# Loading batch 1 ahead of w_in, bringing the first keys as bf16, and cutting the first scores by 384 columns, in a fused attention and feed-forward kernel on one Trainium2 core

## The chip, the cores and the metric

The kernel runs on one core of one Trainium2 chip. The metric is the device time of one execution in microseconds (us), and lower is better. Every execution is listed as undisturbed ("fast"). Kernels are compared only within the same rounds.

A core has five engines with their own instruction streams: TensorE (PE in the profile) for matmuls, ScalarE (ACT) for exponentials, VectorE (DVE), GpSimd (POOL), and SyncE (SP), which only issues transfers. Each engine runs its own stream in program order. Transfers run on 16 DMA engines. A transfer issued by GpSimd can change the type on the way (f32 to bf16), and this queue is called the "cast queue" below.

## The reference, cut to what matters

```python
# q [8,16,384,64], k and v [8,4,384,64], w_in [1024,2048], w_out [2048,1024], all float32
k, v = repeat(k, 4, axis=1), repeat(v, 4, axis=1)   # 16 query heads share 4 key heads
attn = softmax(q @ k.T / 8) @ v                     # per batch and head
x = attn.transpose(0, 2, 1, 3).reshape(3072, 1024)
h = maximum(x @ w_in, 0)
out = (h * h) @ w_out                               # float32 [3072,1024]
```

## The kernel before

One program does attention and feed-forward for 8 batches. The attention of a batch has 4 key groups of 3 key blocks each, 12 units of 128 keys by 4 heads. It first needs k and q transposed ("turned"): kT and qT have the head dimension on the partitions. For batches 0 and 1 the turns run on TensorE against an identity matrix, with a copy by VectorE behind each. From batch 2 on they are transposing transfers. Scores go to PSUM, ScalarE makes exponentials of them, and the product with v ("v product") follows on TensorE. The result is turned once more and goes through w_in ("up" matmuls) and w_out ("down" matmuls).

The program isn't written in its final order. A recorder keeps a model clock for each engine and each queue. At every step the main loop picks the next piece of TensorE work by the model's time at which it would be ready, and among ready pieces by priority. The order of the matmuls is therefore fixed when the program is built. On the chip TensorE then executes that order.

```python
# Recorder.add: what the model believes of a transfer and of an instruction
if dma is not None:
    self.clock[eng] = start + issue
    q = eng
    begin = max(self.ring.get(q, 0.0), start + issue + 0.8)   # queue is serial
    self.ring[q] = begin + cost
    end = begin + cost + 1.2
else:
    self.clock[eng] = start + cost
    end = start + cost + (0.2 if eng == "tensor" else 0.07)
```

The first loads, in the order of the queues:

```python
keys("sync", 0, 1)                       # key group 0 of batch 0 as f32
# ScalarE's queue: q heads 0-3 as f32 (one transfer), then key groups 1-3 as f32
keys("scalar", 1, HKV)
# cast queue (GpSimd), f32 to bf16:
load_q(0, 4, 8)
...                                      # identity matrix
load_v(0)
load_q(0, 8, 12)
load_q(0, 12, 16)
for g in range(1, HKV):
    dup_k(0, "gpsimd", g, g + 1)         # each key block twice side by side, k_dup
aug_v(0, "gpsimd")
for i in range(3):
    load_w_in(i)                         # 1 MB of f32 each, 512 KB as bf16
load_k(1)
load_q(1, 0, 8)
load_q(1, 8, 16)
load_v(1)
for i in range(3, 8):
    load_w_in(i)
dup_k(1, "gpsimd")
aug_v(1, "gpsimd")
```

The scores of batch 0 go in 18 small bursts through two pairs of PSUM banks (1024 columns each, as 2x512 or 2x2x256), each with one exponential of 128x1024. Later batches use bursts with exponentials of 128x3072.

```python
for u in range(NU):
    smalls.append([(u, 0)])
    if u % 2 == 1:
        smalls.append([(u - 1, 512), (u, 512)])
...
# main loop: candidates (model time when ready, priority, what); the lowest priority that is ready wins
if turn_q:
    b, g, w = turn_q[0]
    ...
    cand.append((max(R.when(reads=src), open_bank(spare)), 1, "turn"))
...  # v products 2, turns of the output 3, scores of b0 priority 0, of others 4, up and down 5
ready = [x for x in cand if x[0] <= now + 0.05]
what = min(ready, key=lambda x: x[1]) if ready else min(cand)
```

The softmax here doesn't subtract the row's maximum and nothing guards it: scores larger than these inputs give would overflow.

Of the kernel before, what the change touches and what calls it, by code (L numbers as in the profile page):

```python
# [8 lines left out]
class Recorder:  # L9
# [35 lines left out]
    def add(self, eng, fn, reads=(), writes=(), dma=None, cost=0.1, issue=0.1, rate=None):  # L45
        i = len(self.ops)
# [19 lines left out]
        if dma is not None:  # L66
            self.clock[eng] = start + issue
            q = eng
            begin = max(self.ring.get(q, 0.0), start + issue + 0.8)
            self.ring[q] = begin + cost  # L70
            end = begin + cost + 1.2
        else:
            self.clock[eng] = start + cost
            end = start + cost + (0.2 if eng == "tensor" else 0.07)
# [59 lines left out]
def bass_gqa_attention__then__ffn_squared_relu_kernel(  # L134
# [33 lines left out]
    k_f32 = sb("k_f32", [128, NU, D], f32)  # L168
# [31 lines left out]
    def load_k(b, after=()):  # L200
        st = b % NST
        R.add("gpsimd", lambda g: g.dma_start(  # L202
            k_st[st].ap().rearrange("p (g j) d -> p g (j d)", g=HKV),
            k[b].rearrange("g (p j) d -> p g (j d)", j=NJ)),
            reads=after, writes=[("k_st", st)], dma=f"k{st}", cost=1.3, issue=0.8)

    def first_loads():

        def keys(eng, g0, g1):
            R.add(eng, lambda e: e.dma_start(  # L210
                k_f32[:, g0 * NJ:g1 * NJ, :].rearrange("p (g j) d -> p g (j d)", j=NJ),
                k[0, g0:g1].rearrange("g (p j) d -> p g (j d)", j=NJ)),
                writes=[("k_f32", g) for g in range(g0, g1)], dma=f"kf{g0}", cost=0.4 * (g1 - g0), issue=0.4)

        keys("sync", 0, 1)
        R.add("scalar", lambda e: e.dma_start(
            q_f32[:, :, :], q[0, 0:4].rearrange("h (p j) d -> p h (j d)", j=NJ)),
            writes=["q_f32"], dma="qf", cost=1.3, issue=0.4)
        keys("scalar", 1, HKV)
# [8 lines left out]
    def load_q(b, h0, h1):  # L228
# [4 lines left out]
            writes=[("q_st", st, h // 4, x) for h in range(h0, h1, 4) for x in range(2)], dma=f"q{st}_{h0}",  # L233
# [19 lines left out]
    def dup_k(b, eng, g0=0, g1=HKV):  # L253
        n = (g1 - g0) * NJ
        src = (k_st[b % NST] if b else k_f32)[:, g0 * NJ:g1 * NJ, :].unsqueeze(2).to_broadcast([128, n, 2, D])
        dst = k_dup[b % 2][:, g0 * NJ:g1 * NJ, :, :]
        R.add(eng, lambda e: e.tensor_copy(dst, src), reads=[("k_st", b % NST)] if b else [("k_f32", g) for g in range(g0, g1)],  # L257
# [7 lines left out]
    def turn_k_dma(b):  # L265
# [3 lines left out]
            writes=[("kT", b % 2, g) for g in range(HKV)], dma="turn_k", cost=2.0)  # L269

    def turn_q_dma(b, half):
# [4 lines left out]
            writes=[("qT", b % 2, 2 * half + i, x) for i in range(2) for x in range(2)], dma=f"turn_q{half}", cost=2.5)  # L276
# [16 lines left out]
    def turn_q_pe(b, g, banks, t0=0, t1=6):  # L293
# [3 lines left out]
        parts = [h for h in range(2) if t0 < (4, 6)[h] and t1 > (0, 4)[h]]  # L297

        def tr(pe):
            for t in range(t0, t1):  # L300
# [8 lines left out]
              reads=[("bank", i)], writes=[("qT", b % 2, g, h) for h in parts], cost=0.07 + 0.068 * (t1 - t0))  # L309


    def score_reads(b, u, parts=(0, 1)):
        g = u // NJ
        return [("kT", b % 2, g)] + [("qT", b % 2, g, h) for h in parts]
# [5 lines left out]
    def burst_small(b, pieces, base):  # L320

        wide = 512 // len(pieces)

        def sc(pe):
            for n, (u, c0) in enumerate(pieces):
                for x in range(2):
                    m = pe.matmul(ps[:, base + x, n * wide:(n + 1) * wide],  # L327
                                  kT[b % 2][64 * x:64 * x + 64, u, :], q_cols(b, u // NJ, x, c0, c0 + wide))
            return m

        keys = [("bank", base), ("bank", base + 1)]
        R.add("tensor", sc, reads=[r for u, c0 in pieces for r in score_reads(b, u, (c0 // 512,))], writes=keys,
              cost=0.22 + 0.19)
        n, c0 = (b * NU + pieces[0][0]) % NEX, pieces[0][1]
        src = ps[:, base:base + 2, :].rearrange("p x (k c) -> p x k c", k=len(pieces))
# [370 lines left out]
```

## Time and profile before

| | before |
|---|---|
| median of the first 3 executions | 432.33 us |
| span of the profiled execution | 430.6 us |
| TensorE busy | 421.8 us (98%) |
| first exponential starts, last of the 18 ends | 6.94, 24.43 us |
| first exponential of batch 1 (128x3072) starts | 33.31 us |

The summary page of the kernel before (first line and engine busy times; the last is each engine's busy time, its share and its instructions) says that TensorE is nearly always busy:

```profile
span 430.6 us, 7790 instructions
...
PE 421.8 (98%) x3428; PEld 231.6 (54%) x3454; DVE 158.9 (37%) x335; ACT 194.0 (45%) x190; POOL 55.6 (13%) x68
```

So only the start can give something. The windows table of the kernel before gives, for each stretch, its length and the busy time of each engine with the count of instructions; then the clock that TensorE was granted as the records have it, the DMA share and the GB/s:

```profile
5.00:10.00 5.00, 4.53 (x34) 2.56 (x34) 2.27 (x7) 3.02 (x4) 3.63 (x7) 1.00 1.22 145
10.00:15.00 5.00, 3.65 (x49) 1.84 (x48) 1.86 (x5) 4.56 (x6) 5.00 (x7) 1.00 1.09 139
15.00:20.00 5.00, 4.77 (x80) 2.90 (x76) 3.47 (x11) 5.00 (x7) 4.25 (x5) 1.00 1.47 197
20.00:25.00 5.00, 4.70 (x75) 2.75 (x74) 2.04 (x7) 4.43 (x5) 1.47 (x1) 1.00 1.60 191
25.00:30.00 5.00, 4.50 (x73) 3.54 (x69) 3.99 (x13) 0.98 (x2) 2.61 (x4) 1.00 1.48 198
```

ScalarE's timeline of the kernel before (start, length, engine, line, operation, tiles, count, idle time before with what ended it) shows the 18 exponentials almost gapless:

```profile
6.94 3.08 ACT L337 ACTIVATE expT<-ps 128x1024 bf16<-128x1024 f32 x3 [1.85 <-PE ps L327]
10.33 14.10 ACT L337 ACTIVATE expT<-ps 128x1024 bf16<-128x1024 f32 x15 [0.30 <-PE ps L327]
```

And TensorE's timeline of the kernel before shows what it does between the bursts, and when batch 1 is turned (first and last of four pairs of turns shown; L426 is an up matmul, L285 a turn of k, L301 one of q):

```profile
19.65 0.49 PE L426 MATMUL ps<-xT,w_in_sb 128*128 128x384 bf16 x2
...
20.39 0.50 PE L426 MATMUL ps<-xT,w_in_sb 128*128 128x384 bf16 x2
...
21.15 0.82 PE L426 MATMUL ps<-xT,w_in_sb 128*128 128x384 bf16 x4
...
28.38 0.33 PE L285 MATMUL ps<-ident,k_dup 128*128 128x128 bf16 x3
28.54 0.50 PE L301 MATMUL ps<-ident,q_st 128*128 128x128 bf16 x6
...
29.88 0.33 PE L285 MATMUL ps<-ident,k_dup 128*128 128x128 bf16 x3
30.06 0.51 PE L301 MATMUL ps<-ident,q_st 128*128 128x128 bf16 x6
```

Eight up matmuls (1.3 us at 0.1625 us each) already sit in the gaps at 19.6 to 21.9 us. Batch 1 is turned after the last exponential, from 28.4 to 30.6 us.

### The profile page before, as it was taken

What the parts mean: (1) busy time and instruction counts of PE and PEld (TensorE: products, weight loads), DVE (VectorE), ACT (ScalarE), POOL (GpSimd) and SP (SyncE); (2) the same over time, 40 slices, a digit from 0 to 9 for tenths busy, and PEclk for the clock granted to TensorE, in tenths of its full rate; (3) what the DMA queues carried; (4) which work ended last, traced back from release to release, by engine and by line L of the source; (5) the groups of instructions that cost most, each with busy time, mean ns of one, the idle gap of its engine ahead of it and who ended that gap; (6) DMA issues with size and microseconds to landing.
All of it is one profiled execution on the core that took longest, in us unless ns stands there. A gap on an engine that the chain in (4) does not pass through costs nothing.

```text
span 430.6 us, 7790 instructions
## 1 busy us (share of the span) xinstructions
PE 421.8 (98%) x3428; PEld 231.6 (54%) x3454; DVE 158.9 (37%) x335; ACT 194.0 (45%) x190; POOL 55.6 (13%) x68
## 2 busy tenths in 40 slices
PE   8899999999999999999999999999999999999997
PEld 4465555465454655546555455645564455446544
DVE  3474422254233543225433243533342144224412
ACT  4937750557545576455773549540241034003300
POOL 7752002404040031004000000000000000000000
DMA  8999999999596189299553230042101100110012
GB/s 147 182 195 202 190 198 215 200 191 138 105 175 156 37 137 131 85 144 166 60 103 94 70 85 0 2 106 69 49 2 49 73 26 1 50 73 26 1 63 85
DMA packets 95331, 43.90 MB, mean 102 GB/s; under 512 B 75712, under 2 KB 89280, under 8 KB 95296
## 3 DMA queue, kind: packets, MB, share of 16 engines
q0 software_dynamic: 36544, 17.44, 32.3%
q1 hardware_dynamic: 57824, 25.27, 26.4%
q10 hardware_dynamic: 928, 0.69, 0.5%
q8 instruction: 27, 0.44, 0.4%
q14 instruction: 8, 0.07, 0.1%
HBM read 35.65 MB, written 12.58 MB: 112 GB/s over the span
## 4 chain that ended last, share of the span: by engine, by line
PE 92%; ACT 3%; DMA 2%; DVE 1%; SPq 1%; issue 1%
PE ps L426 39%; PE ps L471 37%; PE ps L347 7%; PE ps L372 7%; ACT expT L337 3%; DMA qT<-q_st 1%; DMA q_f<-in_q_dram 1%; PE ps L301 1%; SPq L266 1%; DVE o_sb L387 1%; PE ps L327 0%; PE ps L285 0%; DVE qT L308 0%; DVE y_sb L480 0%; DVE rinv L381 0%
## 5 line engine op out<-in xcount | busy, mean ns | idle before, releaser
L426 PE MATMUL ps<-xT,w_in_sb 128*128 128x384 bf16 x1024 | 174.5, 326 | 0.0
L471 PE MATMUL ps<-w_out_sb,h2T 128*128 128x512 bf16 (+2 forms) x758 | 167.7, 375 | 1.7 <-issue 0.5
L357 ACT ACTIVATE expT<-ps 128x3072 bf16<-128x3072 f32 x42 | 114.5, 2725 | 70.9 <-PE ps L347 70.0
L426 PEld LDWEIGHTS ps<-xT,w_in_sb 128*128 128x128 bf16 x1024 | 97.0, 98 | 69.3 <-issue 6.2
L436 ACT ACTIVATE h2T<-hr 128x384 bf16<-128x384 f32 x128 | 64.4, 520 | 138.0 <-DVE hr L434 137.8
L471 PEld LDWEIGHTS ps<-w_out_sb,h2T 128*128 128x128 bf16 x784 | 73.6, 98 | 87.9 <-issue 6.0
L434 DVE TENSOR_SCALAR hr<-ps 128x384 f32<-128x384 f32 x128 | 71.2, 557 | 103.9 <-PE ps L426 103.9
L480 DVE COPY y_sb<-ps 128x512 f32<-128x512 f32 (+2 forms) x49 | 33.3, 681 | 130.7 <-PE ps L471 130.7
L372 PEld LDWEIGHTS ps<-v_aug,expT 128*128 128x128 bf16 x1152 | 39.8, 97 | 6.7 <-issue 0.7
L372 PE MATMUL ps<-v_aug,expT 128*128 128x65 bf16 x1152 | 41.4, 193 | 0.3 <-ACT expT L337 0.3
L387 DVE TENSOR_TENSOR o_sb<-ps,rinv 128x384 bf16<-128x384 f32 x64 | 35.6, 557 | 2.4 <-DVE rinv L381 0.2
L347 PE MATMUL ps<-qT,kT 64*128 64x512 bf16 (+1 forms) x336 | 34.6, 325 | 0.5 <-DMA qT<-q_st 0.5
L347 PEld LDWEIGHTS ps<-qT,kT 64*128 64x128 bf16 x336 | 13.0, 94 | 21.2 <-DVE o_sb L387 4.9
L381 DVE RECIPROCAL rinv<-ps 128x6 f32<-128x6 f32 x64 | 12.1, 190 | 25.5 <-PE ps L372 25.5
L337 ACT ACTIVATE expT<-ps 128x1024 bf16<-128x1024 f32 x18 | 16.9, 1070 | 2.4 <-PE ps L327 2.2
L262 POOL COPY v_aug<-v_st 128x768 bf16<-128x768 bf16 x8 | 6.6, 830 | 83.7 <-PE ps L372 67.8
L230 POOL DMA_DIRECT2D q_st<-in_q_dram x17 | 15.0, 896 | 0.9 <-POOLq L691 0.8
L257 POOL COPY k_dup<-k_st 128x1536 bf16<-128x1536 bf16 x7 | 10.3, 1469 | 37.1 <-DMA k_st<-in_k_dram 37.1
L202 POOL DMA_DIRECT2D k_st<-in_k_dram x7 | 5.3, 757 | 39.9 <-DMA qT<-q_st 39.9
L327 PE MATMUL ps<-qT,kT 64*128 64x512 bf16 (+1 forms) x48 | 7.5, 360 | 1.8 <-ACT expT L337 1.3
L240 POOL DMA_DIRECT2D w_in_sb<-in_moe_w_in_dram x8 | 7.1, 935 | 0.0
L223 POOL DMA_DIRECT2D v_st<-in_v_dram x8 | 6.3, 788 | 0.1
(26 smaller groups left out, 42.8 us busy)
## 6 DMA issues: line engine op xcount, KB each, us to landing
out_dram<-y_sb SPq DMA_DIRECT2D x47, 256.0 KB, 2.0
q_st<-in_q_dram POOLq DMA_DIRECT2D x14, 384.0 KB, 8.9
w_in_sb<-in_moe_w_in_dram POOLq DMA_DIRECT2D x8, 512.0 KB, 16.1
w_out_sb<-in_moe_w_out_dram POOLq DMA_DIRECT2D x4, 1024.0 KB, 26.4
v_st<-in_v_dram POOLq DMA_DIRECT2D x8, 192.0 KB, 9.8
k_st<-in_k_dram POOLq DMA_DIRECT2D x7, 192.0 KB, 3.9
q_st<-in_q_dram POOLq DMA_DIRECT2D x3, 192.0 KB, 5.7
xT<-o_sb SPq DMA_TRANSPOSE x28, 2.8
```

What stands on the lines that cost most here:

```text
L230: R.add("gpsimd", lambda g: g.dma_start(q_st[st][:, h0:h1, :], q[b, h0:h1].rearrange("h (p j) d -> p h (j d)", j=NJ)), writes=[("q_st", st ...
L337: R.add("scalar", lambda e: e.activation(dst, src, AF.Exp, scale=0.125), reads=keys, writes=[("expT", (n + m) % NEX, c0 // 512) for m in r ...
L347: m = pe.matmul(flat[:, k0 * HC + c0:k0 * HC + c1], kT[b % 2][64 * x:64 * x + 64, u + k0, :], q_cols(b, (u + k0) // NJ, x, c0, c1))
L357: R.add("scalar", lambda e: e.activation(dst, src, AF.Exp, scale=0.125), reads=keys, writes=[("expT", (n + m) % NEX, h) for m in range(2) ...
L372: m = pe.matmul(po[:, f - 6 * s2, 0:D + 1], w, v_aug[b % 2][:, g * NJ + j, 0:D + 1], start=(j == 0), stop=(j == NJ - 1))
L381: R.add("vector", lambda e: e.reciprocal(rinv[r].ap().unsqueeze(2), po[:, :, D:D + 1]), reads=[("bank", i)], writes=[("rinv", r)], cost=0.13)
L387: R.add("vector", lambda e: e.tensor_tensor(dst, srcv, rbv, ALU.mult), reads=[("bank", i), ("rinv", r)], writes=[("o_sb", o, s2)], cost=0.48)
L426: m = pe.matmul(bank(i)[:, 0:S], w_in_sb[:, kc, c * 128:(c + 1) * 128], xT[b % NXT][:, kc, :], start=(kc == 0), stop=(kc == NKC - 1))
L434: R.add("vector", lambda e: e.tensor_scalar_max(hr[r][:, :], bank(i)[:, 0:S], 0.0), reads=[("bank", i)], writes=[("hr", r)], cost=0.48)
L436: R.add("scalar", lambda e: e.activation(h2T[b % 2][:, c, :], hr[r][:, :], AF.Square), reads=[("hr", r)], writes=[("h2T", b % 2, c)], cost ...
L471: m = pe.matmul(bank(i)[:, 0:n], h2T[b % 2][:, c, i3 * 128:(i3 + 1) * 128], w_out_sb[:, c, c0:c1], start=(c == 0), stop=(c == NFC - 1))
L480: R.add("vector", lambda e: e.tensor_copy(ysl, bank(i)[:, 0:n]), reads=[("bank", i)], writes=[("y", yb)], cost=0.08 + n / 960)
```

## The change

The intent: (1) load k and q of batch 1 ahead of most of w_in, and turn them in the gaps of batch 0; (2) let key groups 1 to 3 of batch 0 come as bf16 through the cast queue, first in that queue, instead of as f32 through ScalarE's queue; (3) load and cast q group 0 by pairs of heads; (4) cut the first and last scores by 384 columns, so that dependencies are finer (16 bursts of 768 and 6 of 1024 in place of 18 of 1024); (5) tell the model that transposing transfers are slow while the cast queue is busy.

```diff
 # Recorder.add
             begin = max(self.ring.get(q, 0.0), start + issue + 0.8)
+            if shared and self.ring.get("gpsimd", 0.0) > begin:
+                self.ring["gpsimd"] += cost
+                cost = shared
             self.ring[q] = begin + cost
-            end = begin + cost + 1.2
+            end = begin + cost + (1.5 if begin > 30 else 1.2)
 # turn_k_dma, turn_q_dma, turn_o_dma
-dma="turn_k", cost=2.0)
+dma="turn_k", cost=1.4, shared=8.0)
 ...
 # first loads
-        R.add("scalar", lambda e: e.dma_start(q_f32[:, :, :], q[0, 0:4]...
-        keys("scalar", 1, HKV)
+        for n in range(2):
+            R.add("scalar", lambda e, n=n: e.dma_start(q_f32[:, 2 * n:2 * n + 2, :], q[0, 2 * n:2 * n + 2]...
 ...
     first_loads()
+    load_k(0)                       # key groups 1-3 of b0, bf16, first in the cast queue
     load_q(0, 4, 8)
     ...
     load_q(0, 12, 16)
-    for g in range(1, HKV):
-        dup_k(0, "gpsimd", g, g + 1)
+    dup_k(0, "gpsimd", 2, 3)
+    load_k(1)
+    dup_k(0, "gpsimd", 3, 4)
+    load_q(1, 0, 8)
     aug_v(0, "gpsimd")
-    for i in range(3):
+    load_q(1, 8, 16)
+    for i in range(2):
         load_w_in(i)
-    load_k(1)
-    load_q(1, 0, 8)
-    load_q(1, 8, 16)
     load_v(1)
-    for i in range(3, 8):
+    for i in range(2, 4):
         load_w_in(i)
     dup_k(1, "gpsimd")
+    for i in range(4, 8):
+        load_w_in(i)
     aug_v(1, "gpsimd")
 ...
     dup_k(0, "vector", 0, 1)
     # casts of q heads 0-1 and 2-3, now both by VectorE
+    dup_k(0, "vector", 1, 2)        # key group 1, ahead of every later VectorE copy
 ...
 # bursts
-        smalls.append([(u, 0)])
-        if u % 2 == 1:
-            smalls.append([(u - 1, 512), (u, 512)])
+        if NJ < u < NU - NJ - 1:
+            ... as before (wide)
+        elif u in (NJ, NU - NJ - 1):
+            smalls += [[(u, 384 * n, 384)] for n in range(2)]
+        elif u % NJ == 0:
+            smalls += [[(u + j, 384 * n, 384)] for n in range(2) for j in range(NJ)]
 ...
-            cand.append((max(R.when(reads=src), open_bank(spare)), 1, "turn"))
+            cand.append((max(R.when(reads=src), open_bank(spare)), 3.5 * b + 1, "turn"))
 # (cut: the bookkeeping of which 128 columns are turned, scored and read, by tiles in place of halves)
```

## The prediction

> **What bounds it now.** The busy table has TensorE busy 421.8 of 430.6 us; the chain of waits is 92% TensorE. From 30 us on it is busy in almost every slice of the windows table (about 2.2 us idle, plus a tail of 2.4). So only the first 30 us can give much. There the timeline shows another bound: ScalarE runs the 18 exponentials of batch 0 from 6.94 to 24.4 us almost gapless (15 took 14.10 us, 0.94 each), and TensorE waits for it. Then come 36 attention-times-v matmuls (1.3 us), the turns of o and 8 up matmuls, and only at 28.2 to 30.5 us are k and q of batch 1 turned: 2.3 us of TensorE work that could have filled the gaps of 10 to 24 us, had the data been there. It stood behind three w_in blocks in the cast queue, which moves 0.19 MB per us.
>
> **What the change does, costed.**
> 1. Turns of batch 1 in the gaps: minus 2.3 us on the critical path. k and q of batch 1 (4.9 us of queue, estimated as 0.98 MB at that rate) now go ahead of w_in. I estimate k landed by 11.5 us, q by 14 to 16, k_dup copied by 17, so the turns fit between 17 and 24 us. VectorE has room: busy 5.5 of 10 us in 15 to 25 us; the eight copies add 4 x (0.35+0.55) = 3.6 us.
> 2. The first w_in block lands at about 18 us instead of 14.9; its first use was 19.6 us. Little or no loss.
> 3. Exponentials by 384 columns: 16 of 128x768 and 6 of 128x1024 instead of 18 of 128x1024. From the two old shapes (1070 and 2725 ns) an element costs 0.81 ns, so the small one takes about 0.73 us: 17.4 against 16.9 us, plus 0.45 us.
> 4. Start: q by head pairs lets the first cast run about 0.6 us earlier. But VectorE executes in order, and the doubling of key group 1 stands before the first kT and qT copies. It waits for the cast queue, which moved its first packet only at about 4.2 us (issued at 1.23). The Trainium skill ("DMA: Bandwidth & Descriptors", the SWDGE anatomy) puts the fixed cost at about 2 us; the trace's 5.4 us to landing for 192 KB decides here. I expect key groups 1-3 at about 5.8 us, and the first exponential at 6.7 to 7.4: perhaps 0.2 us lost.
> 5. Tail of batch 0: the first half of the last group's v product no longer waits for the last exponential (0.5 us), and TensorE fills the rest of the tail with up matmuls and batch 1's first scores (1.2 us together).
> 6. Later stages: same work. The wait for batch 2's transposes (0.5 us at 78 us) may move; plus or minus 1 us.
>
> Sum: -2.3 + 0.45 + 0.2 - 0.5 - 1.2 = about -3.4 us.
>
> **Prediction: 428.9 us, 8 in 10 between 427.2 and 431.2.** Faster by over 2%: 0.02; within 2%: 0.96; slower by over 2%: 0.02.
>
> **What shows it.** Right: batch 1's turns at 16 to 24 us, none at 25 to 31; ScalarE gapless from 7 to 24.6 us; first large exponential (128x3072) at about 26 us instead of 33.3. Step 4 is right if the first kT copy waits on VectorE for k_dup, wrong if the first exponential starts before 6.5 us. Step 2 is wrong if TensorE waits for w_in.
>
> **What would make it wrong.** Bubbles on ScalarE (scores delayed behind turns, two banks for turns and v products); k of batch 1 later than reckoned, so the turns stay in the tail; a stall at 55 to 80 us because batch 1's scores run dry earlier, before batch 2's loads, which haven't moved.

## The result, and the profile after

| | before | after |
|---|---|---|
| median | 432.3 us (432.24 to 432.64, 4 executions) | 433.09 us (433.06 to 433.42, 4 executions) |
| ratio after/before | | 1.0018, 95% interval 1.0001 to 1.0036 |
| profiled span | 430.6 us | 431.6 us |
| first exponential starts, last small one ends | 6.94, 24.43 us | 6.72, 27.09 us |
| first 128x3072 exponential | 33.31 us | 33.34 us |

A ratio here and below is the mean time of one kernel's fast runs over that of the other's of the same rounds, so it isn't quite the ratio of the medians that stand beside it.

The direction was wrong: instead of 3.4 us less, the time is 0.8 us more. The summary page of the kernel after (its granted clock row, in tenths of full speed over 40 slices, did not appear on the page before, in whose trace no change of the clock is recorded; and its chain of waits by line):

```profile
PE 423.4 (98%) x3454; PEld 232.1 (54%) x3454; DVE 159.6 (37%) x337; ACT 193.8 (45%) x193; POOL 55.6 (13%) x68
...
PEclk9899999999999999999999999999999999999999
...
PE ps L426 39%; PE ps L471 39%; PE ps L372 8%; PE ps L347 7%; DMA q_st<-in_q_dram 1%; ACT expT L336 1%; PE ps L326 1%; PE ps L300 1%; PE ps L284 0%; POOL k_st L205 0%; PE ps L405 0%; POOL q_st L229 0%; POOL v_st L222 0%; DVE y_sb L480 0%; POOL ident L498 0%
```

A transfer of q is now a member of the chain, and the second slice (10.8 to 21.6 us) had less than the full clock. The windows table of the kernel after shows the two together:

```profile
5.00:10.00 5.00, 2.33 (x23) 1.15 (x23) 2.49 (x7) 2.92 (x4) 4.45 (x8) 1.00 1.33 145
10.00:15.00 5.00, 3.94 (x41) 2.44 (x41) 1.48 (x3) 2.77 (x4) 5.00 (x7) 0.71 1.55 182
15.00:20.00 5.00, 4.61 (x79) 2.78 (x76) 2.91 (x9) 4.67 (x6) 4.86 (x5) 0.95 1.47 198
20.00:25.00 5.00, 4.40 (x63) 2.48 (x59) 2.64 (x8) 5.00 (x8) 1.43 (x2) 1.00 1.48 195
25.00:30.00 5.00, 5.00 (x89) 4.06 (x88) 3.80 (x12) 2.09 (x3) 5.00 (x7) 1.00 1.46 198
```

From 5 to 15 us TensorE was busy 6.27 us, against 8.18 us before; ScalarE 5.69 against 7.58. The timelines of TensorE and of ScalarE in the kernel after, around the hole:

```profile
8.29 0.34 PE L326 MATMUL ps<-qT,kT 64*128 64x384 bf16 x2
11.06 0.49 PE L300 MATMUL ps<-ident,q_st 128*128 128x128 bf16 x6 [2.44 <-DMA q_st<-in_q_dram]
11.49 0.50 PE L326 MATMUL ps<-qT,kT 64*128 64x384 bf16 x4
```

```profile
6.72 2.92 ACT L336 ACTIVATE expT<-ps 128x768 bf16<-128x768 f32 x4 [3.69 <-PE ps L326]
11.87 1.51 ACT L336 ACTIVATE expT<-ps 128x768 bf16<-128x768 f32 x2 [2.23 <-PE ps L326]
```

TensorE stands 2.44 us before a turn of q, waiting for its data. The scores that follow (the fifth burst, of key group 0 and of query heads that were turned long ago) need none of that data, but they stand behind the turn in program order, so ScalarE runs dry for 2.23 us. The chain of waits of the kernel after, in order of time (start, length, what), names the transfer:

```profile
3.75 0.75 POOL v_st L222
4.50 6.43 DMA q_st<-in_q_dram
10.93 0.14 issue
11.06 0.49 PE ps L300 x6
```

This is q heads 8 to 11, issued at 4.50 and landed at 10.93 us. The model's landing time for it was 9.04 us. In the kernel before the same transfer was modelled at 7.99 and landed at 9.15 us, and nothing waited for it:

```profile
9.29 0.67 PE L301 MATMUL ps<-ident,q_st 128*128 128x128 bf16 x6
```

That turn doesn't stand later in the order there: it comes after three bursts of 1024 columns, in the kernel after behind four of 768. But its data came 1.8 us earlier, and TensorE, still at half speed there though the clock column says 1.00, reached it only at 9.29 us.

The cast queue delivers later, with 144 KB of keys ahead in it. It moved 0.51 MB from 4 to 8 us (128 GB/s), and the keys are 0.15 MB. At that rate they account for an estimated 1.15 us of the 1.78 us by which the landing is later; the rest is not explained. The pages' lists of transfers (out, in, engine, count, size, median us from issue to landing) have for the three 192 KB pieces of q of batch 0, first the kernel before, then the kernel after:

```profile
q_st<-in_q_dram POOLq DMA_DIRECT2D x3, 192.0 KB, 5.7
```

```profile
q_st<-in_q_dram POOLq DMA_DIRECT2D x3, 192.0 KB, 6.4
```

And batch 1's turns, which should have gone between 17 and 24 us? TensorE's timeline of the kernel after (first and last pair):

```profile
26.59 0.33 PE L284 MATMUL ps<-ident,k_dup 128*128 128x128 bf16 x3
26.75 0.50 PE L300 MATMUL ps<-ident,q_st 128*128 128x128 bf16 x6
...
29.41 0.34 PE L284 MATMUL ps<-ident,k_dup 128*128 128x128 bf16 x3
29.68 0.51 PE L300 MATMUL ps<-ident,q_st 128*128 128x128 bf16 x6
```

They moved by less than 2 us. Meanwhile only 2 of the 8 early up matmuls were left in the gaps before 25 us; the first w_in block now lands at 20.2 us in place of 14.8.

To compare the early stage by one number, "work by 42 us" adds up what TensorE had finished by then, from the counted weight loads times the full-speed cost of each kind (up 0.1625, v product 0.0312, turn 0.0565, batch 1's scores 0.095 us; batch 0's scores, the same in all, left out). Before has 24.10 us, after 22.64. So 1.46 us were lost early. About 0.5 came back later: a wait of 0.45 us at 77.9 us for a transposing transfer of batch 2's q is gone after the change (from 30 to 90 us TensorE was busy 59.34 us before and 60.00 after). Together that is the 1.0 us by which the spans differ.

This number is of one execution. In 17 of the 20 profiles below, span plus work by 42 us is 454.0 to 454.3 us, so it decides the span of its own execution (the other three, before, e4 and i1, waited 0.45, 1.88 and 0.89 us for transposes of batch 2 later). But two profiles of one kernel differ in it by 0.16 (h1 and i1), 0.32 (after and f1), 0.65 (f2 and i2) and 1.13 us (g1 and i3). A difference of about 1 us between two kernels' single profiles is therefore no proof.

### The profile page after: what moved, and what is told of

The parts are those of the page before. It is cut to its first block, busy times and chain, and to the rows that moved or that the text cites. A ratio compares the mean times of both kernels' runs of the same rounds, so it can differ in the third digit from the quotient of the medians.

```text
span 431.6 us, 7821 instructions
## 1 busy us (share of the span) xinstructions
PE 423.4 (98%) x3454; PEld 232.1 (54%) x3454; DVE 159.6 (37%) x337; ACT 193.8 (45%) x193; POOL 55.6 (13%) x68
## 3 DMA queue, kind: packets, MB, share of 16 engines
q1 hardware_dynamic: 57824, 25.27, 26.7%
## 4 chain that ended last, share of the span: by engine, by line
PE 95%; DMA 1%; ACT 1%; POOL 1%; issue 0%; DVE 0%; POOLq 0%
PE ps L426 39%; PE ps L471 39%; PE ps L372 8%; PE ps L347 7%; DMA q_st<-in_q_dram 1%; ACT expT L336 1%; PE ps L326 1%; PE ps L300 1%; PE ps L284 0%; POOL k_st L205 0%; PE ps L405 0%; POOL q_st L229 0%; POOL v_st L222 0%; DVE y_sb L480 0%; POOL ident L498 0%
## 5 line engine op out<-in xcount | busy, mean ns | idle before, releaser
L471 PE MATMUL ps<-w_out_sb,h2T 128*128 128x512 bf16 (+2 forms) x784 | 171.8, 375 | 0.0
L372 PE MATMUL ps<-v_aug,expT 128*128 128x65 bf16 x1152 | 42.8, 194 | 0.0
L347 PE MATMUL ps<-qT,kT 64*128 64x512 bf16 (+1 forms) x336 | 34.6, 325 | 0.0
L336 ACT ACTIVATE expT<-ps 128x768 bf16<-128x768 f32 (+1 forms) x22 | 17.4, 872 | 6.6 <-PE ps L326 6.5
L256 POOL COPY k_dup<-k_st 128x1536 bf16<-128x1536 bf16 (+1 forms) x9 | 11.4, 1268 | 37.4 <-PE ps L372 34.4
L326 PE MATMUL ps<-qT,kT 64*128 64x384 bf16 (+2 forms) x48 | 7.9, 354 | 0.8 <-ACT expT L336 0.6
L300 PE MATMUL ps<-ident,q_st 128*128 128x128 bf16 x48 | 4.7, 236 | 3.7 <-DMA q_st<-in_q_dram 2.4
```

What stands on the lines that cost most here:

```text
L326: mm = pe.matmul(ps[:, base + x, m * wide:(m + 1) * wide], kT[b % 2][64 * x:64 * x + 64, u, :], q_cols(b, u // NJ, x, c0, c0 + wide))
L336: R.add("scalar", lambda e: e.activation(dst, src, AF.Exp, scale=0.125), reads=keys, writes=[("expT", (b * NU + u) % NEX, t) for u, _, _ i ...
L347: m = pe.matmul(flat[:, k0 * HC + c0:k0 * HC + c1], kT[b % 2][64 * x:64 * x + 64, u + k0, :], q_cols(b, (u + k0) // NJ, x, c0, c1))
L372: m = pe.matmul(po[:, f - 6 * s2, 0:D + 1], w, v_aug[b % 2][:, g * NJ + j, 0:D + 1], start=(j == 0), stop=(j == NJ - 1))
L471: m = pe.matmul(bank(i)[:, 0:n], h2T[b % 2][:, c, i3 * 128:(i3 + 1) * 128], w_out_sb[:, c, c0:c1], start=(c == 0), stop=(c == NFC - 1))
```

## The experiments

All eighteen runs gave correct results. The theory after the first reading was theory O: the loss is the wait in program order for q heads 8 to 11, caused by wrong modelled landing times. The rivals were that the narrow bursts, the late first exponential, the half-speed clock, or batch 1's loads cost the time.

| run | edit in a few words | ratio to before (95%) | median us | profile: first exponential starts / last small one ends / first 128x3072 | work by 42 us |
|---|---|---|---|---|---|
| before | | | 432.3 | 6.94 / 24.43 / 33.31 | 24.10 |
| after | | 1.0018 | 433.09 | 6.72 / 27.09 / 33.34 | 22.64 |
| e1_order | model told the landings | 0.9988 (0.9943 to 1.0032) | 432.14 | 7.75 / 25.53 / 31.78 | 24.05 |
| e2_warm | 20 filler matmuls in the wait | 1.0049 (1.0013 to 1.0085) | 434.51 | 7.72 / 27.85 / 34.11 | 21.6 |
| e3_first | batch-1 part undone | 1.0053 (1.0017 to 1.0089) | 434.99 | 7.44 / 26.21 / 32.31 | 22.04 |
| e4_batch1 | batch-1 part alone | 1.0026 (0.9979 to 1.0072) | 433.19 | 6.90 / 23.62 / 30.88 | 24.86 |
| f1_again | after, unchanged | 1.0007 (0.9993 to 1.0021) | 432.5 | 7.19 / 26.51 / 32.77 | 22.96 |
| f2_order_start | e1 + key group 1 doubled later | 0.9987 (0.9974 to 1.0000) | 431.52 | 5.79 / 25.20 / 31.44 | 24.37 |
| f3_plan | e1 + measured copy costs | 1.0026 (1.0011 to 1.0040) | 433.29 | 7.51 / 27.78 / 31.70 | 22.23 |
| f4_plan_start | f3 + f2's start | 1.0009 (0.9994 to 1.0023) | 432.87 | 6.01 / 27.17 / 31.58 | 22.75 |
| g1_batch1_dma | e4 + the model's transposes | 0.9979 (0.9967 to 0.9992) | 431.06 | 6.44 / 23.40 / 30.65 | 25.18 |
| g2_batch1_plan | g1 + measured copy costs | 1.0001 (0.9982 to 1.0021) | 431.95 | 6.52 / 24.72 / 29.42 | 24.86 |
| g3_warm | f2 + fillers in ten bursts | 1.0008 (0.9996 to 1.0021) | 432.54 | 6.01 / 25.73 / 31.98 | 23.72 |
| g4_plan_warm | f4 + the same fillers | 1.0029 (1.0015 to 1.0044) | 433.27 | 5.74 / 26.89 / 31.30 | 22.91 |
| h1_wide | f2 + before's wide bursts | 0.9985 (0.9964 to 1.0007) | 430.51 | 6.39 / 23.00 / 29.50 | 26.32 |
| h2_keys_f32 | keys 1-3 as f32 again | 1.0021 (1.0007 to 1.0035) | 432.89 | 6.07 / 25.22 / 31.45 | 24.37 |
| h3_keys_wide | h2 + wide bursts but for the last group | 1.0018 (1.0006 to 1.0030) | 432.64 | 6.61 / 26.08 / 32.33 | 23.53 |
| i1_wide_again | h1_wide, unchanged | 0.9958 (0.9934 to 0.9983) | 430.46 | 6.50 / 23.15 / 29.65 | 26.16 |
| i2_narrow_again | f2, unchanged | 0.9992 (0.9964 to 1.0020) | 432.08 | 5.70 / 25.85 / 32.10 | 23.72 |
| i3_batch1_again | g1, unchanged | 0.9986 (0.9961 to 1.0012) | 431.75 | 6.90 / 24.42 / 31.68 | 24.05 |

### e1_order: the model told when v and q land

```diff
 # load_v
-cost=1.3, issue=0.8)
+cost=1.3 if b else 2.5, issue=0.8)
 # load_q
-cost=0.33 * (h1 - h0), issue=0.8)
+cost=0.33 * (h1 - h0) + (0.7 if (b, h0) == (0, 8) else 0.0), issue=0.8)
```

> The changed kernel, with only the planner's clock corrected for two loads (v and q heads 8-12 of batch 0 land at 8.9 and 10.9 us as measured, not at 7.7 and 9.0), so that TensorE's program order puts the remaining scores of key group 0 before the turn of q heads 8-12. Theory A (that turn, early in program order and waiting for its load, is what ate the gain): TensorE no longer idle from 8.6 to 11.1 us, ScalarE without the 2.2 us gap, granted clock 1.0 at 10 to 15 us, time about 430.6 us (2.5 less than the changed kernel's 433.1). Rival B (the many small exponentials and the late w_in set the end of the first stage anyway): 432.5 to 433.3 us. The turns of batch 1 stay at 25 to 29 us under both.

Measured: ratio 0.9988, median 432.14 against 431.97 us for before in these rounds, which were noisy (before reached 434.99). In the profile no wait of TensorE for q is left, though the transfer still lands at 10.86 us, and ScalarE's timeline has no gap from 9.58 us on:

```profile
9.58 15.95 ACT L336 ACTIVATE expT<-ps 128x768 bf16<-128x768 f32 x20 [0.32 <-PE ps L326]
```

TensorE's work by 42 us is back at 24.05 us, the level of before. Nothing but two numbers of the model changed, and no transfer changed its place in its queue. So the two waits in the profile of after did come from the order behind the late transfer; that part of theory O is shown. That they cost all of the 1.4 us is not: this profile also lacks the half-speed period from 12.13 to 15.54 us, and the noisy ratio tells nothing apart. And it brings only a tie with before, not the predicted gain.

### e2_warm: filler matmuls while TensorE waits

```diff
+def keep_warm(pe):
+    for _ in range(20):
+        m = pe.matmul(bank(7)[:, 0:256], warm[:, 0:128], warm[:, :])
+    return m
 # just before the turn of q group 2, with cost 0 in the model
+R.add("tensor", keep_warm, reads=["warm"], writes=[("bank", 7)], cost=0.0)
```

> The changed kernel, with 20 idle-time matmuls on zeros put in front of the waiting turn of q heads 8-12, which keep TensorE busy for about 2.1 us of its 2.4 us wait. It separates the wait from the low granted clock that follows it (0.71 at 10 to 15 us). Theory A (the wait itself costs most): clock 1.0 at 10 to 15 us, but ScalarE's gap stays at 2.0 us or more, time 432.3 to 432.8. Rival C (the clock after the wait costs most): 431.5 or less.

A miss. The clock had already fallen when the fillers began (it was granted 0.5 from 8.1 to 11.5 us), so they took longer than the wait that they should fill. The timeline of TensorE in this run:

```profile
9.89 3.15 PE L535 MATMUL ps<-warm 128*128 128x256 bf16 x20
12.87 0.50 PE L300 MATMUL ps<-ident,q_st 128*128 128x128 bf16 x6
```

They made the order's cost larger, and the run says nothing of what the half clock costs by itself.

### e3_first: the batch-1 part of the change undone

```diff
 # GpSimd's order again: doubles of groups 2 and 3, aug_v, w_in 0-2, k1, q1, q1, v1, w_in 3-7, doubles and aug_v of batch 1
-3.5 * b + 1, "turn"
+1, "turn"
```

> The changed kernel with its second half undone: w_in ahead of batch 1's k and q again, batch 1's turns first in priority again; the new first loads and narrow exponentials kept. Theory A: q heads 8-12 still land after 9.8 us and TensorE's planned order still waits for them, so the ScalarE gap stays (1.2 us or more), and the time is 432.8 to 434.0, no better than the changed kernel. Rival D (loading batch 1 early is what costs): below 431.8. If q heads 8-12 land about 1 us earlier than 10.9, the issue of batch 1's loads is what slowed the cast queue at 6 to 8 us.

The time rose to 1.0053. q heads 8 to 11 landed at 10.94 us, as in the kernel after (10.93), and TensorE waited 0.98 us for them (ScalarE's gap was 0.94 us, less than theory A's 1.2). So batch 1's loads are not what delays this transfer. Whatever comes behind it in the queue doesn't matter; the keys ahead of it are what is left. Taking batch 1's part away did not make the kernel faster, so that part isn't the harm either.

### e4_batch1: the batch-1 part alone, on the kernel before

```diff
 # on before: GpSimd's order
+dup 1-3, load_k(1), load_q(1,0,8), aug_v(0), load_q(1,8,16), w_in 0-1, load_v(1), w_in 2-3, dup_k(1), w_in 4-7, aug_v(1)
-1, "turn"
+3.5 * b + 1, "turn"
```

> The kernel before, with only the second half of the change: k and q of batch 1 ahead of w_in and turned at low priority in gaps of batch 0; first loads and exponentials as before. Theory A: no ScalarE gap over 0.5 us in 7 to 24 us; the turns come at about 22 to 27 us, because the planner reckons the k_dup copy of batch 1 at 4.0 us instead of the measured 1.5; time 430.5 to 431.8, less than before (432.3) but not the full 2.3 us. Rival D (early batch 1 loads delay w_in and cost time): 432.5 or more.

The early stage gained (work by 42 us 24.86), but a wait much later took it back. TensorE's timeline of this run:

```profile
76.68 0.82 PE L347 MATMUL ps<-qT,kT 64*128 64x512 bf16 x8 [1.88 <-DMA qT<-q_st]
```

Scores of batch 2 stand in the order ahead of down matmuls that were ready, and wait 1.88 us for a transposing transfer (0.45 us in the kernel before). This is the same kind of fault as the q wait: the model took the transposes for faster than they are. The change has a line for it (`shared`), which this kernel lacked.

### f1_again: the kernel after, unchanged

> The changed kernel itself, unchanged, on the chip and in the rounds of the next three, so that they can be compared with it: 433 us and 1.001 to 1.004 of the kernel before. TensorE's 2.4 us wait for q heads 8-12 must be seen again. Open: whether key groups 1-3 land at 5.3 us as in its first profile or at 6.1 to 6.4 as in the two experiments of the last call; the first exponential then starts at 6.7 or 7.7 us.

Ratio 1.0007 (0.9993 to 1.0021), 431.6 to 433.65 us. By the two ratios the change is a tie or a loss of 0.1 to 0.2%; it is never the 0.8% gain that was predicted. The expected wait of 2.4 us for q did not come back in full. TensorE's timeline of this run:

```profile
6.54 0.34 PE L300 MATMUL ps<-ident,q_st 128*128 128x128 bf16 x3 [2.00 <-DVE kT L289]
10.43 0.80 PE L300 MATMUL ps<-ident,q_st 128*128 128x128 bf16 x6 [0.75 <-DMA q_st<-in_q_dram]
```

The transfer landed at 10.29 us here, and TensorE came later to the turn: it had lost 2.00 us at the start, behind the wait of VectorE for key group 1 (step 4), and the clock was halved from 7.28 to 14.10 us. Yet work by 42 us is 22.96 us, nearly as low as in the first profile (22.64). So the wait for q is not the whole loss. This run was also the first in which the executions of one kernel could be sorted by their mean granted clock: three at 0.992 took 432.86, 432.88 and 433.65 us (mean 433.13), three at 1.0 took 431.6, 431.79 and 432.14 us (mean 431.84). More on this below.

### f2_order_start: e1 and a start without the wait for key group 1

```diff
 # on e1: VectorE doubles key group 1 after the first copies of kT and qT
-    dup_k(0, "vector", 1, 2)                 # before the loop
+            if (b, g, w) == (0, 0, "c"):
+                dup_k(0, "vector", 1, 2)     # after the turn of the second half of q group 0
```

> As e1_order, and VectorE doubles key group 1 after the first qT copies instead of before the first kT copy. Theory E (the in-order wait of VectorE for the cast queue is a second loss, as step 4 of the prediction has it): first exponential at 5.8 to 6.3 us instead of 7.75 in e1_order, narrow exponentials gapless, the last one ending near 24 us instead of 25.5, time 1.2 to 1.8 us below e1_order's ratio of 0.999, so about 0.9955 of before (430.3). Rival F (the stage ends when w_in and batch 1's data come, not when the exponentials end): within 0.5 us of e1_order.

The first exponential starts at 5.79 us (7.75 in e1). So VectorE's order was indeed what held the start back, though part of these 2 us is TensorE's speed: e1 ran at half speed until 10.19 us, its first recorded change of the clock. But the ratio is 0.9987, against 0.9988 for e1, and the last small exponential ends only 0.33 us earlier than in e1. An earlier start was turned into new gaps: in this profile the granted clock is 0.5 from 11.83 to 15.24 us, and bursts there take 0.61 instead of 0.39 us.

### f3_plan and f4_plan_start: measured costs of copies in the model

```diff
 # on e1 (f3) and on f2 (f4)
-0.33 * n                      # dup_k by GpSimd
+(1.45 if n == NU else 0.5)
-2.0                           # aug_v
+0.8
-cost=total / 2400 + 0.2       # a small burst
+cost=total / 2400 + 0.03
```

> As e1_order, and the planner also reckons with measured durations: k_dup of batch 1 1.45 us (it had 4.0), narrow k_dup 0.5 (1.0), v_aug 0.8 (2.0), and 0.17 us less of TensorE per score burst. Only the program order changes. Theory G (the turns of batch 1 stayed in the tail because the planner thought their data late and TensorE full): turns at about 17 to 25 us, first 128x3072 exponential at about 28 us instead of 31.8 in e1_order, time 1.0 to 2.0 us below e1_order, ratio about 0.995 to 0.997. Rival H (there is no room in the gaps; turns there only delay the exponentials by as much): within 0.5 us of e1_order.

> Both edits together. If theories E and G hold and add up: ratio 0.9915 to 0.9940 of before (428.6 to 429.7), near what was predicted for the change; last narrow exponential at about 24 us, first 128x3072 exponential at 26.5 to 27.5 us. If only one of them holds, it equals the better of the last two.

Both are slower than the kernels that they were made from: 1.0026 against 0.9988, and 1.0009 against 0.9987. The last small exponential ends 2.0 to 2.25 us later. With "better" costs the model puts the turns earlier, and they delay the scores and thereby ScalarE. Both profiles also show two half-speed periods (8.10 to 14.93 us, and 9.79 to 16.61 us), so the two causes are mixed in these runs. What they do show is that earlier turns are no gain by themselves.

### g1_batch1_dma: the batch-1 part with the model's new transpose costs

```diff
 # on e4: the "shared" block of the change in Recorder.add, and
+turn_k_dma cost=1.4, shared=8.0; turn_q_dma cost=2.5, shared=8.0; turn_o_dma cost=0.9, shared=6.0
```

> As e4_batch1 (only batch 1's early loads and low-priority turns added to the kernel before), plus the planner's new reckoning of transposes by DMA while the cast queue runs, which the changed kernel also has. e4_batch1 gained at the start (first 128x3072 exponential 30.9 against 33.3 us) but lost 1.9 us waiting for batch 2's q transposes at 75 us. Expected if that wait is only one of program order: no TensorE wait over 0.3 us at 60 to 90 us, span about 429.2, ratio 0.9965 to 0.998. If the wait stays, the ratio stays at 1.002.

The wait at 76.7 us is gone, and the ratio is 0.9979 with its interval below 1 (430.72 to 431.56 us, six executions). So the batch-1 part is worth about 0.2%, or 0.9 us, once the model knows the transposes. That includes the wait of 0.45 us at 77.9 us in the kernel before, which is gone too; only the rest can be due to the turns.

### g2_batch1_plan: batch 1's turns forced into the gaps

```diff
 # on g1: the costs of f3 for dup_k and aug_v, and a small burst
-cost=0.22 + 0.19
+cost=0.24
```

> As g1_batch1_dma, and the planner reckons with the measured durations of the copies on GpSimd and 0.17 us less of TensorE per score burst. Here the TensorE clock is up from 5 us on, which f3_plan and f4_plan_start lacked, so it is a clean test. Theory G (batch 1's turns fit in the gaps once the planner knows the data are there): turns from 18 to 24.5 us, first 128x3072 exponential at 27 to 28.5 us, ratio about 0.994 (1.2 us or more below g1). Rival H (no room: turns delay exponentials as much): within 0.5 us of g1.

The turns of batch 1 now run from 19.3 to 26.7 us, most of them where the prediction wanted them. The ratio is 1.0001: no gain over before, and about 0.2% worse than g1 (medians 431.95 and 431.06 us). The last small exponential ends at 24.72 us in place of 23.40. From 15 to 25 us TensorE was idle 1.36 us in g1 and 0.70 us in g2. So the turns filled 0.7 us of idle time and pushed bursts back for the rest of their 2.3 us.

### g3_warm and g4_plan_warm: fillers against the half clock

```diff
 # in burst_small, for the third to the twelfth burst, on f2 (g3) and on f4 (g4)
+3 filler matmuls of 128x256 ahead of the scores, cost 0 in the model
```

> As f2_order_start, with three matmuls of 256 columns on zeros ahead of each of ten narrow score bursts at 7 to 15 us, where TensorE had waited for ScalarE. Theory J (the sparse stream of narrow bursts lets the granted clock fall to 0.5 for one or two periods of 3.4 us, and TensorE at half clock then holds up ScalarE): clock 1.0 at 5 to 20 us, last narrow exponential at about 24 us instead of 25.2, ratio 0.995 to 0.9965 (f2: 0.9987). Rival K (half clock is hidden behind ScalarE): within 0.4 us of f2, or slower by the added matmuls.

> As f4_plan_start, with the same added matmuls. f4_plan_start had the clock at 0.5 at 10 to 16.6 us and its last narrow exponential at 27.2 us. Theories G and J together: clock 1.0, last narrow exponential at about 24.2 us, first 128x3072 exponential at 27 us, ratio 0.992 to 0.9945. If J holds and G doesn't: like g3_warm. If J falls: 1.000.

The recorded clock stayed at 1.00, but three fillers took 0.49 us and stood in front of scores that were ready. The ratios are 1.0008 and 1.0029, both 0.002 above the kernels without fillers. Inconclusive for the cost of the clock: what the halved clock costs can't be told from what the fillers cost.

### h1_wide: the change with the old wide bursts

```diff
 # on f2
-... 16 bursts of 768 columns and 6 of 1024
+        smalls.append([(u, 0, 512)])
+        if u % 2 == 1:
+            smalls.append([(u - 1, 512, 256), (u, 512, 256)])
```

> As f2_order_start (ratio 0.9987), with batch 0's scores and exponentials again in 18 bursts of 1024 columns instead of 22 of 768 and 1024. Theory L (narrow bursts cost: 0.45 us of ScalarE, and more where TensorE runs at half clock): last narrow exponential near 24.5 us instead of 25.2 although the first starts 0.4 us later, ratio 0.997 to 0.998. Rival M (narrow bursts are neutral or help by finer overlap): 0.9985 to 1.000.

The profile was the best of all: 18 exponentials in 16.61 us without a gap, the last ending at 23.0 us, work by 42 us 26.32, span 427.8 us. The six timed executions fell on two values, four at 429.6 to 430.6 and two at 432.6, so the ratio of 0.9985 didn't tell it apart from f2. It was therefore repeated (i1).

### h2_keys_f32 and h3_keys_wide: the keys back in their old queue

```diff
 # on after (h2): key groups 1-3 as f32 by ScalarE's queue as its third transfer, doubled by GpSimd
-    load_k(0)
-    dup_k(0, "vector", 1, 2)
+    dup_k(0, "gpsimd", 1, 2)
 # h3: also wide bursts in key groups 0-2, narrow ones in the last
```

> The changed kernel with one element undone: keys 1-3 of batch 0 come again as f32 by ScalarE's queue, and nothing of them stands in the cast queue. Theory A': q heads 8-12 land at about 9.2 us as in the kernel before (10.9 in the changed one), v about 1 us earlier, no wait of TensorE over 0.7 us for them, first exponential at about 6 us since VectorE waits for no cast load, ratio 0.9975 to 0.999. If the ratio stays at 1.000 or more, the keys' way in is not what loses.

> As h2_keys_f32, and wide bursts for key groups 0 to 2, narrow only for the last one. If theories A' and L hold: the best so far, ratio 0.9955 to 0.9975, last narrow exponential at 23.0 to 23.6 us. If the narrow last group and the head pairs bring nothing over g1_batch1_dma: 0.998.

With the keys out of the cast queue, q heads 8 to 11 land at 9.33 us and the wait for them is gone without any change to the model's numbers. That is the direct test of what made them late. The other profiles agree, but for h3 (9.95 us): 8.3 to 9.2 us in the five others without these keys in the queue, 9.9 to 10.9 us in the thirteen with them. But the time doesn't fall (1.0021 and 1.0018); now the keys are late. Nor do h3's wide bursts change anything against h2 here (medians 432.64 and 432.89 us). TensorE's waits in h2 from 5 to 15 us (us in total, times, longest):

```profile
PE ps L288 <- POOL k_dup L260: 1.5, 1, 1.5
```

One wait was swapped for another: as the third transfer of ScalarE's queue the keys were issued at 1.75 us and landed at 7.2 us; as the second, in the kernel before, they were issued at 1.23 us and landed at about 6.6 us.

### i1_wide_again, i2_narrow_again, i3_batch1_again: repeats on one chip

No edits: the kernels of h1_wide, f2_order_start and g1_batch1_dma.

> The kernel of h1_wide unchanged. Theory N (narrow bursts themselves cost time, since they leave TensorE no slack): ratio 0.995 to 0.998 and a lower median than the narrow kernel of the same call, by 0.8 us or more, in most executions. Rival Z (burst width is worth nothing; h1_wide's profile was a lucky execution): within 0.4 us of the narrow kernel. If the two values of h1_wide come back (about 430 and about 432.6), the spread is the kernel's own.

> The kernel of f2_order_start unchanged, for the comparison on one chip. Both theories: ratio 0.997 to 1.000.

> The kernel of g1_batch1_dma unchanged. If the batch-1 part with the planner's new transpose cost is a real gain: ratio 0.997 to 0.999 again, with the interval below 1. If the first result was luck: 0.999 to 1.001.

With wide bursts the five executions took 430.18 to 430.67 us, ratio 0.9958 (0.9934 to 0.9983). With narrow ones, on the same chip and in the same rounds, the median is 432.08 us and the ratio 0.9992. So in this call the narrow bursts cost about 1.6 us by the medians (1.0 us between h1 and f2, from two calls on another chip, with ratios that don't differ). The edit changes the model's costs too, and with them the order, so this is the price of the bursts with their order. The two values of h1_wide did not come back; why two of its executions took 432.6 us stays open. i3 gives 0.9986, the same side as g1's 0.9979, but its interval includes 1. So 0.1 to 0.2% for the batch-1 part was seen twice and was outside the error once. In the profiled execution of i3 the clock was halved from 7.25 to 10.67 us, and its work by 42 us is no more than that of before, in place of g1's 25.18: of its 0.6 us less span, the wait at 77.9 us is most.

Where do the narrow bursts lose? Not in ScalarE's own time (e1: 15.95 us for 20 of them, near the rate that was predicted). The timelines of ScalarE, first i1 (wide), then i2 (narrow):

```profile
6.50 16.65 ACT L336 ACTIVATE expT<-ps 128x1024 bf16<-128x1024 f32 x18 [3.46 <-PE ps L326]
```

```profile
5.70 1.51 ACT L336 ACTIVATE expT<-ps 128x768 bf16<-128x768 f32 x2 [2.68 <-PE ps L326]
8.41 3.63 ACT L336 ACTIVATE expT<-ps 128x768 bf16<-128x768 f32 x5 [1.20 <-PE ps L326]
12.42 1.73 ACT L336 ACTIVATE expT<-ps 128x768 bf16<-128x768 f32 x2 [0.38 <-PE ps L326]
14.46 1.02 ACT L336 ACTIVATE expT<-ps 128x1024 bf16<-128x1024 f32 x1 [0.32 <-PE ps L326]
15.89 9.96 ACT L336 ACTIVATE expT<-ps 128x1024 bf16<-128x1024 f32 x12 [0.41 <-PE ps L326]
```

And the windows of i1, then of i2 (the clock is the third number from the right):

```profile
5.00:10.00 5.00, 3.21 (x27) 1.33 (x27) 2.21 (x7) 3.50 (x4) 4.75 (x8) 1.00 1.37 152
10.00:15.00 5.00, 4.47 (x78) 2.99 (x79) 2.71 (x7) 5.00 (x7) 5.00 (x7) 1.00 1.51 171
```

```profile
5.00:10.00 5.00, 3.16 (x27) 1.33 (x27) 2.22 (x6) 3.10 (x5) 4.46 (x8) 0.86 1.37 154
10.00:15.00 5.00, 4.80 (x37) 2.60 (x38) 1.47 (x3) 4.30 (x6) 5.00 (x7) 0.50 1.46 165
```

From 10 to 15 us both are busy, but the narrow kernel got 37 matmuls done where the wide one got 78 (of another mix, with v products already): its clock was halved for two periods (8.57 to 15.40 us). Just before, TensorE of i2 had waited 1.07 us for the doubled keys of group 1, which i1 did not, so burst width is not the only difference of the two profiles. The executions sorted by mean granted clock say the same in time (a mean of 0.992 is 3.4 us of lost clock in 431 us, i.e. two halved periods of 3.41 us):

| kernel (all that had both) | mean us at 0.992 (executions) | mean us at 1.0 (executions) |
|---|---|---|
| after, first run | 433.09 (2) | 433.06 (1) |
| after, f1_again | 433.13 (3) | 431.84 (3) |
| e1_order | 432.54 (2) | 431.44 (2) |
| e3_first | 435.13 (3) | 434.08 (1) |
| e4_batch1 (wide) | 433.48 (1) | 432.70 (2) |
| f2_order_start | 432.16 (2) | 430.97 (1) |
| f3_plan | 433.52 (2) | 433.18 (4) |
| f4_plan_start | 433.01 (4) | 431.00 (1) |
| h3_keys_wide (wide but for the last group) | 432.64 (1) | 432.77 (3) |
| i2_narrow_again | 432.14 (4) | 430.45 (1) |

Seven of the ten pairs differ by 0.8 to 2.0 us; the other three by 0.34, 0.03 and -0.13 us. Of the eleven executions of the narrow kernel (f2 and i2), nine had a mean below 1.0, six of them 0.992; of the eleven of the wide kernel (h1 and i1), two had 0.996 and none 0.992. The one full-clock execution of i2 took 430.45 us, the same as the wide kernel's median. So the sorting points to the clock for the larger part of what the narrow bursts lose; of the narrow kernel it rests on two executions at full clock (i2's and f2's 430.97 us).

Two limits of this. It sorts executions; nothing forced the clock. And the recorded clock reads 1.00 until its first recorded change, also where matmuls plainly run slower: in the profile of before, three turns take 0.50 us at 7.27 and at 8.89 us and 0.34 at 10.22 us. So "1.0" includes executions that began at half speed: the profiles of e1 and e3 are listed with 1.0, and their first recorded change, to full clock, comes at 10.19 and 10.26 us. That may be why three pairs don't separate; it was not tested. It also means that the kernel before, whose profile began like this, is not known to have had the same clock as the kernels it is compared with.

## Why the prediction was wrong

**What bounds it: right for the most part.** In the chain of waits of the kernel before, ScalarE's small exponentials stand from 11.5 to 24.4 us, and TensorE after that. Before 11.5 us it is the first load of q and TensorE's own turns and scores, which the prediction did not see.

**Step 1, batch 1's turns in the gaps (minus 2.3 us): the failed step of the sum.** "So the turns fit between 17 and 24 us" is not so. The windows table of before had 0.53 us of idle TensorE from 15 to 25 us, and those gaps already held 8 up matmuls. The prediction took "TensorE waits for ScalarE" for free room and never added the room up: 2.3 us do not fit into 0.5. In the kernel after, the turns ran at 26.6 to 30.2 us, although batch 1's doubled keys were ready at 16.4 us and its q at 17.1: the model reckoned that copy at 4.0 us where it took 1.5, and TensorE as fuller than it was. But with these costs put right (f3, g2) nothing was gained; where the turns started at 19.3 us (g2), the exponentials were pushed back by 1.3 us and the ratio was 1.0001. The part done alone, with the turns where they fit, measured 0.1 to 0.2% (g1, i3): about 0.6 to 0.9 us in place of 2.3, with the 0.45 us of the later wait in it.

**The missed cost: the order of TensorE's program.** The prediction put the bf16 keys at the head of the cast queue and asked what they delay on VectorE (step 4). It did not ask what they delay in the cast queue itself, nor what the model believes of it. q heads 8 to 11 landed at 10.93 us where the model had 9.04, and a turn that waits for them stands ahead of ready scores: TensorE idle 2.44 us, ScalarE 2.23. "Bubbles on ScalarE" stood in the list of what would make the prediction wrong, and "scores delayed behind turns" is what came, by a late load. e1 and h2 removed the wait in two different ways, and e3 showed that batch 1's loads have no part in it. In the second profile of the change (f1) the wait was 0.75 us, beside 6.8 us at half speed. How the loss divides between the wait, the start and the halved clock was not separated.

**Step 3, exponentials by 384 columns (plus 0.45 us): right on ScalarE, wrong in total.** 20 of them ran in 15.95 us in e1, close to the rate predicted. But the narrow kernel is 1.6 us slower than the wide one by the medians of i1 and i2, and by the sorting of executions the larger part of it comes with the halved clock, which the prediction did not consider.

**Step 2, w_in later, no loss: half right.** TensorE never waits for w_in. But block 0 lands at 20.2 us in place of the predicted 18, and six of the eight up matmuls (1.0 us) left the gaps. Batch 1's turns did not take their place; they came still later (26.6 us).

**Step 4, the start: right.** VectorE waited 0.67 us for key group 1, the copies of kT and qT stood behind it, and the first exponential started at 6.72 us (7.19 in f1_again), within the predicted 6.7 to 7.4. Without this wait (f2, i2) the start came at 5.79 and 5.70 us, and the time changed by nothing that could be measured.

**Step 5, the tail (minus 1.7 us): not separated.** From the last small exponential to the first large one took 8.88 us before and 6.25 us after, so the tail did shrink by 2.6 us. But the last small exponential came 2.66 us later, which ate all of it: the first large exponential started at 33.34 us against 33.31 before, and the predicted 26 us was reached by no kernel (29.42 us in g2 at best). The early stage as a whole could not give 3.4 us by filling gaps, when the idle time from 5 to 30 us was 2.85 us (the half-speed time before 10 us counted as busy).

**Step 6, later stages: right.** The wait at 77.9 us went away (plus 0.5 us for the change), within the margin of 1 us.

**The sum.** After against before: 1.46 us of TensorE work lost by 42 us, 0.5 won back later, 1.0 us longer in the profile, 0.8 us by the medians. With the order and the start repaired and the wide bursts kept, the same change is 1.4 us faster than before by the medians (430.46 against 431.89 us, ratio 0.9958). In h1 the same kernel had 0.9985, with an interval that includes 1. This is the best kernel, and it lies inside the predicted range of time, but not by the predicted steps: its turns of batch 1 run from 20.0 to 26.5 us, and it is without the narrow bursts. So the range was met by luck.

**Skill pages that the argument rests on.** The Trainium skill, "TensorE: Matmul & The Clock Gate", Part 1, says that TensorE's clock is halved when it isn't busy and that activity is judged in windows of 3413 ns. The trace agrees: the halved periods were 3.41 us long or twice that (12.13 to 15.54 us in the kernel after, 8.57 to 15.40 us in i2). The same page, in "HAM oscillation — how this bites in real kernels", gives the rule of no idle gaps of more than about 3.4 us. This differs: the longest idle time in the window before the clock fell was 2.44 us in the kernel after and 1.07 us in i2. "DMA: Bandwidth & Descriptors", in the anatomy of the SWDGE path, gives 2.0 us plus bytes at 436 GB/s, an estimate of 2.45 us for 192 KB. The traces have 5.7 us (before) and 6.4 us (after) in the queue at the start, so the formula for one transfer does not serve for a queue of them.

**What stays open.** What the halved clock costs by itself was not forced in any run (e2, g3 and g4 spoiled it). Why two of h1_wide's executions took 432.6 us is not known. And the effect of the bf16 keys alone, with a right model, was not separated from the head pairs.

## What to carry to other kernels

Before crediting work with moving "into the gaps", add up the idle time of the engine that is to do it, in exactly the window named: a gain can't be larger than that, and work that already fills the gaps is pushed out. When an order is fixed at build time from modelled landings, every transfer put at the head of a queue changes what lands behind it, and one late input ahead of ready work stops two engines; compare modelled and measured landing times after each such change. And where an engine's clock follows its activity, smaller pieces can cost more than their own overhead; sort the executions of one kernel by granted clock before explaining a difference under 1%.

## What the Trainium skill lacked or had wrong

- "TensorE: Matmul & The Clock Gate" (Part 1 and "HAM oscillation") ties the fall to half clock to an idle window of about 3.4 us. A later section, "A second HAM failure mode", has a clock that swings with frequent short pauses, but none gives a share of busy time. Here, in the 3.41 us before the recorded fall, TensorE had been busy for 31% (after), 35% (e2), 41% (f1_again, f3), 55% (i3), 56% (h2), 58% (i2), 62% (f2) and 66% (f4) by the matmul times of the traces. Windows of 67% (h1), 68% (after, i1), 69% (g2), 71% (f2) and once 63% (i3) were not followed by a fall. So the limit seen here is near two thirds busy, not complete idleness; the ends of matmuls in the traces are modelled, so the share is rough.
- The same page warns that the trace's records of the clock can be unreliable, but says nothing of what this profiler shows before the first recorded change: in the profile of before it reads 1.00, where three 128-column turns take 0.50 us at 7.27 us and 0.34 us at 10.22 us. The durations show half speed where the record doesn't.
- "DMA: Bandwidth & Descriptors" (anatomy of the SWDGE path) has a cost for one transfer; none of the pages read gives one for several casting transfers queued at the start of a kernel, where 192 KB took 5.7 to 6.4 us from issue to landing and the queue moved 128 GB/s from 4 to 8 us.
